# Two early expert tiles in plain float32, and where the split of second weights stands

## The chip, the cores and the metric

The kernel runs on one core of one Trainium2 chip. The metric is the device time of one execution in microseconds (us); lower is better. Of the core's engines the text uses TensorE (PE, with its weight loads PEld), VectorE (DVE), ScalarE (ACT), GpSimd (POOL) and SyncE (SP, which here only issues DMA transfers).

## The reference

Three stages follow each other: a block-causal attention, a dense squared-relu layer, and a mixture of experts that sends each token to one of eight experts. The change lies in the third:

```python
logits = x @ w_gate + modality_bias[modality_id]   # x: 2304 x 512, 8 experts
e_idx = np.argmax(logits, axis=1)
gate_w = probs[np.arange(N), e_idx]                # softmax of logits
for e in range(E):
    mask = e_idx == e
    h = np.maximum(x[mask] @ w1[e], 0.0)           # w1[e]: 512 x 1024, first product
    out[mask] = gate_w[mask, None] * (h @ w2[e])   # w2[e]: 1024 x 512, second product
```

## The kernel before

**Float32 in three products.** Matmuls run on the types `F32` or `F32R`. For most products the kernel splits each float32 operand into a high part (a cast to `F32R`, on ACT) and a low part (the difference, on DVE), and adds up three `F32R` matmuls, high x high, high x low and low x high (`PASSES`, line 498). For a transposed activation `hilo` (924) does this. For weights it is `split` (897), made of `high` (903, ACT, line 904) and `low` (906, DVE, line 910). A whole expert is eight raw weight tiles of 128x1024, `raw[0..3]` for w1 and `raw[4..7]` for w2, each 512 KB. As soon as `low` is through with a raw tile it issues the load of the next token tile's weights into the same place (`load`, 866, on SP's queue). That load has a condition: it moves data only when the next tile has another expert; otherwise it is issued and skipped.

**Token tiles.** The router (`Router`, 501) counts the tokens per expert and packs them into token tiles of 128 rows of one expert. The plan has 17 such tiles (`PLANNED`). The rows that are left over go into six small tiles (32 or 64 rows, `small`, 990), which use plain float32 matmuls and have raw buffers of their own, `raw_s`; their loads are unconditional, and the first tile's eight (`load_small(0, a)`, 887) wait until the gather of the second steady tile has landed (`self.gathered`).

**Two early tiles.** The last block of the dense layer is routed only when its rows are done. Two tiles (`EARLY`, tiles 0 and 1) are chosen before, by `early` (686), from the other tokens of the busiest expert. Their weights are loaded while the dense layer ends: w1 on SP's queue, w2 on POOL's. Then `finish` (747) works out all other tiles on DVE: it ends with `ei` (each tile's expert, 817 and 818), which SP reads before it can issue a conditional load, and `gidx` (the rows to gather, 802), which POOL reads for its gathers (`gather`, 915).

**Order of the work.** `run` (1073) puts the instructions of PE, ACT and DVE in the order in which they are traced (`manual_schedule`); the router's instructions, and those of SP and POOL, are put in between or in order by a scheduler that simulates the kernel. `issue_after(ins)` queues what its block traces on `ins`'s engine behind `ins`; it adds nothing on other engines. The dependency tracker makes a reader of a tile wait for the last instruction before it in traced order that writes the tile, a DMA included.

For the two early tiles `run` splits w1 into high and low, runs tile 0's first product with the matmuls on high weights first (`turns`, 937), lets the parts of the low split wait behind marked points of the router (`acc`, `sel`, `base`, `items`, `index`), runs tile 1's first product, then tile 0's second, then tile 1's second. After them `steady` (1045) works on one tile per turn: first product of tile i, second product of tile i-1, transposes between.

Of the kernel before, what the change touches and what calls it, by code (L numbers as in the profile page):

```python
# [9 lines left out]
F32 = mybir.dt.float32  # L10
# [3 lines left out]
AF = mybir.ActivationFunctionType  # L14
ALU = mybir.AluOpType
AX = mybir.AxisListType
PSUM = bass.MemoryType.PSUM
P = 128
# [260 lines left out]
class SquaredRelu:  # L279
# [54 lines left out]
    def low(self, f, h, l, eng):  # L334
        eng.tensor_sub(l, f, h.bitcast(F32))
# [147 lines left out]
EARLY = 2  # L483
# [14 lines left out]
PASSES = ((0, 0), (0, 1), (1, 0))  # L498


class Router:
# [7 lines left out]
    def __init__(self, nc, persist, ident, modality_id, w_gate, modality_bias, x2_d):  # L509
        self.nc, self.ident, self.x2_d = nc, ident, x2_d  # L510
        NT = x2_d.shape[0]
        D, E = w_gate.shape
        self.NT, self.D, self.E = NT, D, E
        self.NJ = NT // P
        self.NI = NT // P + E - 1
        self.src = (modality_id, w_gate, modality_bias)
        t = lambda n, sh, dt=F32: persist.tile(sh, dt, name=n)
        self.NA = self.NI + TINY + SMALL
        self.gidx = t("gidx", [P, self.NA], I32)
        self.sidx = t("sidx", [P, self.NA], I32)  # L520
        self.ei = t("ei", [1, 2, self.NA], I32)
        self.used = t("used", [1, 1], I32)
        self.gidx_e = t("gidx_e", [P, EARLY], I32)
        self.sidx_e = t("sidx_e", [P, EARLY], I32)
        self.ee = t("ee", [1, 1], I32)
        self.last = {}

    def open(self, ctx, tc, ps, lead):

# [84 lines left out]
    def block(self, blk, rows):  # L614

        nc, E, D, wk = self.nc, self.E, self.D, self.wk
        w = lambda n, sh, dt=F32: wk.tile(sh, dt, name=n, tag=n)
# [33 lines left out]
        oh = self.oh[:, n0:n0 + 2]  # L651
        nc.vector.tensor_tensor(oh, bc(self.down), bc(m2), ALU.is_equal)
        for n in range(2):
            self.last["acc"] = nc.vector.tensor_add(self.acc[:, n0 + n + 1], self.acc[:, n0 + n], self.oh[:, n0 + n])
        yield
        pr = self.ps.tile([P, 2, E], F32, name="pr", tag="g", padded_shape=[P, 64, E])
        nc.tensor.matmul(pr, self.tri, oh, start=True, stop=False)
# [9 lines left out]
        nc.vector.tensor_copy(lo, ri[:, 0])  # L667
        nc.vector.tensor_copy(self.hi[:, n0:n0 + 2], ri[:, 1])
        for e in range(2):
            self.last["sel"] = nc.vector.tensor_scalar(self.A[n0 + e], self.col, lo[:, e:e + 1], None, ALU.is_equal)  # L670
        ex, sm = w("ex", [P, 2, E]), w("sm", [P, 2])
        nc.vector.tensor_sub(ex, lg, bc(m))
        nc.scalar.activation(ex, ex, AF.Exp)
# [73 lines left out]
    def finish(self, ctx, tc):  # L747
# [28 lines left out]
        left = t("left", [P, 1, E])  # L776
        v.tensor_sub(left, tiles, self.less)
        base = self.before("base", left)
        self.last["base"] = v.tensor_scalar_add(base, base, float(EARLY))
        end, zero = t("cend", [P, 1, E]), t("zero", [P, 1, E])  # L780
        v.tensor_add(end, base, left)
        v.tensor_sub(zero, base, self.less)
# [9 lines left out]
        Bm = self.wk.tile([P, NJ, 3, NA], BF16, name="Bm", tag="Bm")  # L792
        v.tensor_tensor(Bm[:, :, 0], self.item.to_broadcast(sh), it.to_broadcast(sh), ALU.is_equal)
        v.tensor_mul(Bm[:, :, 1], Bm[:, :, 0], self.tile_no.to_broadcast(sh))
        self.last["items"] = v.tensor_scalar_mul(Bm[:, :, 2], Bm[:, :, 0], self.part)
        pb = self.ps.tile([P, 3, NA], F32, name="pb", tag="g")
        for j in range(NJ):
            nc.tensor.matmul(pb, self.A[j], Bm[:, j], start=(j == 0), stop=(j == NJ - 1))
        u, w, z = t("tk", [P, NA]), t("tk2", [P, NA]), t("tk3", [P, NA])
        v.tensor_copy(u, pb[:, 2])  # L800
        v.scalar_tensor_tensor(u, pb[:, 1], float(P), u, ALU.mult, ALU.add)
        self.last["index"] = v.tensor_copy(self.gidx, u)
        v.tensor_scalar(w, pb[:, 0], -8192.0, 8192.0, ALU.mult, ALU.add)
        v.tensor_add(z, u, w)
        self.token(self.sidx, z, w)
# [15 lines left out]


class Experts:

# [70 lines left out]
    def split(self, i, a, c, end):  # L897
        if i >= end:
            return
        self.high(a, c)  # L900
        self.low(i, a, c, end)

    def high(self, a, c):
        self.nc.scalar.copy((self.w1s, self.w2s)[a][0][c], self.raw[4 * a + c])  # L904

    def low(self, i, a, c, end, after=None):

        ws, r = (self.w1s, self.w2s)[a], self.raw[4 * a + c]
        with self.tc.issue_after(self.rt.last[after].ins) if after else nullcontext():
            self.nc.vector.tensor_sub(ws[1][c], r, ws[0][c].bitcast(F32))  # L910
        i = max(i + 1, EARLY)
        if i < end:
            self.load(i, a, c)

    def gather(self, i, rows):
        rt, nc = self.rt, self.nc
# [17 lines left out]
            nc.vector.tensor_sub(l[:, s], pt, h[:, s].bitcast(F32))  # L934
        return h, l

    def turns(self, i, n):


        if i == 0:  # L940
            return sorted(((c, a, w) for c in range(n) for a, w in PASSES), key=lambda t: t[2])
        return [(c, a, w) for c in range(n) for a, w in PASSES]

    def hidden(self, i, xT, end):
        nc, KD = self.nc, self.KD
        ph = self.ps_h.tile([P, 2, 512], F32, name="ph", tag="h")
        for t, (c, a, w) in enumerate(self.turns(i, KD)):
            for n in range(2):
                nc.tensor.matmul(ph[:, n], xT[a][:, c], self.w1s[w][c][:, n * 512:(n + 1) * 512],  # L949
                                 start=(t == 0), stop=(t == 3 * KD - 1))  # L950
            if i >= EARLY and t % 3 == 2:
                self.split(i + 1, 0, c, end)
        h = self.hp.tile([P, self.F], F32, name="h", tag="h")
        for n in range(2):
            nc.scalar.activation(h[:, n * 512:(n + 1) * 512], ph[:, n], AF.Relu)
        return h

    def project(self, i, hT, xr, end, between=None):
        nc, D, KF = self.nc, self.D, self.KF
        if i == end - 1:  # L960
            py = self.rt.ps.tile([P, D], F32, name="py", tag="g")
        else:
            py = self.ps_y.tile([P, D], F32, name="py", tag="y")
        for t, (c, a, w) in enumerate(self.turns(i, KF)):
            nc.tensor.matmul(py, hT[a][:, c], self.w2s[w][c // 2][:, c % 2 * D:c % 2 * D + D],  # L965
                             start=(t == 0), stop=(t == 3 * KF - 1))
            if t == 3 * KF // 2 and between:
                between()
            if t % 6 == 5 and i >= EARLY - 1:
                self.split(i + 1, 1, c // 2, end)  # L970
        y = self.sb.tile([P, D], F32, name="y", tag="y")
        nc.scalar.mul(y, py, xr[:, D:D + 1])
        self.scatter(i, y, self.rt.sidx_e if i < EARLY else self.rt.sidx)

    def scatter(self, i, y, idx):
        n = y.shape[0]
# [65 lines left out]
        for j in range(TINY + SMALL):  # L1042
            yield from self.small(j)

    def steady(self, i0, end, xs, xT, before=None, steps=iter(())):

        for i in range(i0, end + 1):
            if i < end:
                h = self.hidden(i, xT.pop(i), end)
            if i == i0 and i + 1 < end and i + 1 not in xT:  # L1050
                xT[i + 1] = self.hilo("x", xs[i + 1], self.KD)
            next(steps, None)
            turn = lambda: self.hilo("h", h, self.KF)
            if before and i == end - 1:
                for _ in steps:
                    pass
                hT = []
                self.project(*before, xs.pop(i - 1), end, lambda: hT.extend(turn()))
                before = i, hT
                continue  # L1060
            if before:
                self.project(*before, xs.pop(i - 1), end)
            for n in range(i + 2, min(i + 4, end)):
                if n not in xs:
                    xs[n] = self.gather(n, self.NT)
            next(steps, None)
            if i < end:
                before = i, turn()
            next(steps, None)
            if i + 2 < end:  # L1070
                xT[i + 2] = self.hilo("x", xs[i + 2], self.KD)

    def run(self):
        nc, tc, KD, KF = self.nc, self.tc, self.KD, self.KF
        i0, end = EARLY, PLANNED
        self.engines = set([mybir.EngineType.PE, mybir.EngineType.Activation, mybir.EngineType.DVE])
        xs, xT = self.xs, {}
        for i in (i0, i0 + 1):
            xs[i] = self.gather(i, self.NT)
        self.gather_small(0)  # L1080
        with tc.manual_schedule(engines=self.engines):
            with tc.high_priority():
                for c in range(4):
                    self.high(0, c)
            xT[0] = self.hilo("x", xs[0], KD)
            for c in range(4):
                self.low(0, 0, c, end, (None, None, "acc", "sel")[c])
            xT[1] = self.hilo("x", xs[1], KD)
            for c in range(4):
                self.high(1, c)  # L1090
            h0 = self.hidden(0, xT.pop(0), end)
            with tc.issue_after(self.rt.last["base"].ins):
                hT0 = self.hilo("h", h0, KF)
            for c in range(4):
                self.low(0, 1, c, end, "index" if c else "items")
            for a in range(2):
                self.load_small(0, a)
            h1 = self.hidden(1, xT.pop(1), end)
            self.project(0, hT0, xs.pop(0), end)
            hT1 = self.hilo("h", h1, KF)  # L1100
            for c in range(4):
                self.split(i0, 0, c, end)
            self.project(1, hT1, xs.pop(1), end, lambda: xT.update({i0: self.hilo("x", xs[i0], KD)}))
            self.steady(i0, end, xs, xT, None, self.smalls())
        self.rest(end, 1)

    def rest(self, i0, n):
# [129 lines left out]
```

## Time and profile before

| | |
|---|---|
| Time, median of 3 runs | 938.98 us (938.69 to 939.5) |
| The profiled execution's own time | 940.87 us |
| Its span in the trace | 939.2 us |
| PE busy | 899.4 us (96%) |
| DVE busy | 600.0 us (64%) |
| ACT busy | 524.1 us (56%) |
| POOL busy | 211.8 us (23%) |

The span runs from the first instruction to the last of one execution; the execution's own time is 1.67 us longer, and 1.89 us above the median of the runs. A busy matmul engine is not one at its peak, since matmuls overlap: a matmul's duration is longer than its distance to the next, and where a rate is wanted, start times are compared.

### The profile page before, as it was taken

Reading aid. Unit: us, or ns where it says so; the run is one execution under the profiler, and the core shown is the slowest. Engines: PE = TensorE matmul, PEld = TensorE weight load, DVE = VectorE, ACT = ScalarE, POOL = GpSimd, SP = SyncE. Lnnn points to the kernel's source line nnn. Section 1 sums busy time; section 2 is a strip of 40 time slices with the busy share of each in tenths; the row PEclk is TensorE's granted clock in tenths of the full one; section 3 lists DMA queues with packets and bytes.
Section 4 is the critical chain, followed back from the end, with each engine's and each line's share of the span. In section 5 each row is a group of like instructions: output and inputs, shape, how many; then the busy total and the mean of one; then the engine's idle time right before and its main releaser. Section 6 shows DMA issues by size and latency. Waiting matters only on the chain. (4 is left out here: it accounts for less than half of the span.)

```text
span 939.2 us, 16334 instructions
## 1 busy us (share of the span) xinstructions
PE 899.4 (96%) x5553; PEld 727.2 (77%) x5553; DVE 600.0 (64%) x1376; ACT 524.1 (56%) x1109; POOL 211.8 (23%) x319
## 2 busy tenths in 40 slices
PE   7989999999999999999999999999889999999995
PEld 5666777787878788999988888887667776766774
DVE  4888876373645445777344444445987887776762
ACT  6878786575756543333222222224377786776763
POOL 4576656133333200000000000002041321222110
PEclk9999999999999999999999999999999999999998
DMA  6465553221321133446012222115173696537400
GB/s 145 133 170 134 161 163 78 76 68 57 73 84 36 50 115 109 135 138 200 23 68 68 69 68 68 46 46 196 52 249 116 231 385 227 210 123 270 159 24 25
DMA packets 109477, 113.79 MB, mean 121 GB/s; under 512 B 62679, under 2 KB 80617, under 8 KB 109387
## 3 DMA queue, kind: packets, MB, share of 16 engines
q1 hardware_dynamic: 105579, 100.74, 34.1%
q0 software_dynamic: 3808, 11.94, 3.6%
q8 instruction: 46, 0.75, 0.3%
q14 instruction: 44, 0.36, 0.1%
HBM read 143.58 MB, written 19.80 MB: 174 GB/s over the span
## 5 line engine op out<-in xcount | busy, mean ns | idle before, releaser
L377 PE MATMUL ph<-xh,wih 128*128 128x256 f32 x576 | 162.9, 283 | 0.0
L377 PE MATMUL ph<-xh,wil 128*128 128x256 f32 x576 | 162.5, 282 | 0.0
L377 PE MATMUL ph<-xl,wih 128*128 128x256 f32 x576 | 162.3, 282 | 0.0
L160 POOL TENSOR_TENSOR p<-p,rc 128x64 f32<-128x64 f32 (+2 forms) x144 | 111.1, 779 | 140.0 <-DVE rc L159 71.2
L381 ACT ACTIVATE r<-ph 128x512 f32<-128x512 f32 x72 | 43.0, 597 | 163.3 <-PE ph L377 138.1
L382 DVE SCALAR_TENSOR_TENSOR r<-r,sc 128x512 f32<-128x512 f32 x72 | 55.8, 775 | 93.6 <-ACT r L381 89.8
L377 PEld LDWEIGHTS ph<-xh,wih 128*128 128x128 f32 x576 | 109.1, 189 | 3.5 <-ACT r L381 0.9
L377 PEld LDWEIGHTS ph<-xl,wih 128*128 128x128 f32 x576 | 109.3, 190 | 2.3
L377 PEld LDWEIGHTS ph<-xh,wil 128*128 128x128 f32 x576 | 109.3, 190 | 0.1
L142 DVE TENSOR_REDUCE nm<-sc 128x1 f32<-128x288 f32 (+8 forms) x160 | 70.7, 450 | 54.8 <-PE sc L140 44.4
L147 ACT ACTIVATE p<-sc,nm 128x288 f32<-128x288 f32 (+8 forms) x160 | 80.4, 505 | 24.2 <-DVE nm L142 10.6
L910 DVE TENSOR_TENSOR w2l<-raw,w2h 128x1024 fp32r<-128x1024 f32 x64 | 77.4, 1223 | 13.9 <-ACT w2h L904 12.8
L910 DVE TENSOR_TENSOR w1l<-raw,w1h 128x1024 fp32r<-128x1024 f32 x64 | 76.8, 1223 | 14.2 <-ACT w1h L904 13.6
L392 PE MATMUL px<-woh,gh 128*128 128x512 f32 x200 | 81.6, 408 | 0.0
L392 PE MATMUL px<-woh,gl 128*128 128x512 f32 x200 | 78.6, 394 | 0.0
L392 PE MATMUL px<-wol,gh 128*128 128x512 f32 x200 | 78.5, 393 | 0.0
L904 ACT CAST w1h<-raw 128x1024 fp32r<-128x1024 f32 x64 | 65.6, 1049 | 16.7 <-PE ph L949 15.3
L919 POOL DMA_INDIRECT xr<-x_d,gidx_e x2 | 2.3, 1129 | 317.0 <-DMA raw<-in_moe_w_dram 316.7
L904 ACT CAST w2h<-raw 128x1024 fp32r<-128x1024 f32 x64 | 66.5, 1049 | 12.4 <-PE py L965 11.3
L385 ACT ACTIVATE gh<-r,sc 128x512 fp32r<-128x512 f32 x72 | 52.2, 725 | 34.1 <-DVE r L382 34.1
L179 PE MATMUL tp<-ident,p 128*128 128x128 f32 x400 | 65.9, 280 | 5.4 <-POOL p L160 3.7
L185 ACT COPY pt<-tp 128x512 f32<-128x512 f32 (+3 forms) x128 | 61.6, 497 | 9.2 <-PE tp L179 8.6
(269 smaller groups left out, 1982.2 us busy)
## 6 DMA issues: line engine op xcount, KB each, us to landing
raw<-in_moe_w_dram SPq DMA_DIRECT2D x172, 512.0 KB
xr<-xT_d SPq DMA_DIRECT2D x19, 512.0 KB
wr<-in_moe_w_in_dram SPq DMA_DIRECT2D x16, 512.0 KB
wr<-in_moe_w_out_dram SPq DMA_DIRECT2D x16, 512.0 KB
row<-part_d SPq DMA_DIRECT2D x20, 256.0 KB
x_d<-row SPq DMA_DIRECT2D x18, 256.5 KB
xT_d<-x SPq DMA_DIRECT2D x16, 288.0 KB
raw_q<-in_q_dram SPq DMA_DIRECT2D x32, 128.0 KB
```

Source lines behind the costliest of these rows:

```text
L142: ps.last["max"] = nc.vector.tensor_reduce(nm[:, e:e + 1], sc[:, 0:w], AX.X, ALU.max, negate=True)
L147: ps.last["exp"] = nc.scalar.activation(pr[:, k0:k0 + w], scs[e][:, 0:w], AF.Exp, bias=nm[:, 0:1], accum_out=sm[:, e:e + 1])
L160: ps.last["scale"] = nc.gpsimd.tensor_mul(pr[:, 0:n], pr[:, 0:n], rc.to_broadcast([P, n]))
L179: nc.tensor.transpose(t[:, e * P:(e + 1) * P], st[u][i][0][:, c * P:(c + 1) * P], ident)
L185: P_COPY(nc, i0)(o, src)
L377: nc.tensor.matmul(ph[:, e], self.wi[p][w][:, c, e * P:(e + 1) * P], x[a][:, c], start=(n == 0), stop=(n == 3 * KC - 1))
L381: nc.scalar.activation(r, ph, AF.Relu)
L382: nc.vector.scalar_tensor_tensor(r, r, self.sc[:, 0:1], r, ALU.mult, ALU.mult)
L385: nc.scalar.activation(gh, r, AF.Identity, bias=self.sc[:, 1:2])
L392: self.nc.tensor.matmul(px, g[a][:, e, t * P:(t + 1) * P], self.wo[p][w][:, e], start=(first and e == 0 and n == 0), stop=(last and e == 1 ...
L904: self.nc.scalar.copy((self.w1s, self.w2s)[a][0][c], self.raw[4 * a + c])
L910: self.nc.vector.tensor_sub(ws[1][c], r, ws[0][c].bitcast(F32))
```

## The change

The classes' parts that mark points in the router (`self.last[...]`) go, except the one behind `gidx`. The core of the rest:

```diff
     def split(self, i, a, c, end):
...
-        self.high(a, c)
-        self.low(i, a, c, end)
...
+        self.nc.scalar.copy(ws[0][c], r)
+        self.nc.vector.tensor_sub(ws[1][c], r, ws[0][c].bitcast(F32))
+        if i + 1 < end:
+            self.load(i + 1, a, c)
...
+    def plain(self, nm, src, n):
+        o = self.sb.tile([P, n, P], F32, name=nm + "f", tag=nm + "h")
+        for g in range(n // 4):
+            pt = (self.ps_t if nm == "h" else self.ps_u).tile([P, 4, P], F32, name="pt" + nm, tag="t")
+            for c in range(4):
+                self.nc.tensor.transpose(pt[:, c], src[:, (4 * g + c) * P:(4 * g + c + 1) * P], self.ident)
+            self.nc.scalar.copy(o[:, 4 * g:4 * g + 4], pt)
+        return o
+
+    def hidden_early(self, xT):
...
+        for c in range(KD):
+            for n in range(2):
+                nc.tensor.matmul(ph[:, n], xT[:, c], self.raw[c][:, n * 512:(n + 1) * 512],
+                                 start=(c == 0), stop=(c == KD - 1))
+        return self.relu(ph)
+
+    def project_early(self, i, hT, xr, between=None):
...
+        for c in range(KF):
+            nc.tensor.matmul(py, hT[:, c], self.raw[4 + c // 2][:, c % 2 * D:c % 2 * D + D],
+                             start=(c == 0), stop=(c == KF - 1))
...
+        self.result(i, py, xr)
...
     def project(self, i, hT, xr, end, between=None):
...
-            if t % 6 == 5 and i >= EARLY - 1:
+            if t % 6 == 5 and i >= EARLY:
                 self.split(i + 1, 1, c // 2, end)
...
     def steady(...):
...
             if i < end:
                 before = i, turn()
+            if i == i0 and w2:
+                for c in range(4):
+                    self.split(i, 1, c, end)
...
     def run(self):
...
-            with tc.high_priority():
-                for c in range(4):
-                    self.high(0, c)
-            xT[0] = self.hilo("x", xs[0], KD)
-            for c in range(4):
-                self.low(0, 0, c, end, (None, None, "acc", "sel")[c])
-            xT[1] = self.hilo("x", xs[1], KD)
-            for c in range(4):
-                self.high(1, c)
-            h0 = self.hidden(0, xT.pop(0), end)
-            with tc.issue_after(self.rt.last["base"].ins):
-                hT0 = self.hilo("h", h0, KF)
-            for c in range(4):
-                self.low(0, 1, c, end, "index" if c else "items")
+            for i in range(2):
+                xT[i] = self.plain("x", xs[i], KD)
+            h0 = self.hidden_early(xT.pop(0))
+            hT0 = self.plain("h", h0, KF)
+            h1 = self.hidden_early(xT.pop(1))
+            for c in range(4):
+                self.load(i0, 0, c)
             for a in range(2):
                 self.load_small(0, a)
-            h1 = self.hidden(1, xT.pop(1), end)
-            self.project(0, hT0, xs.pop(0), end)
+            with tc.issue_after(self.rt.last.ins):
+                for c in range(4):
+                    self.split(1, 1, c, end)
+            self.project_early(0, hT0, xs.pop(0))
             hT1 = self.hilo("h", h1, KF)
             for c in range(4):
                 self.split(i0, 0, c, end)
             self.project(1, hT1, xs.pop(1), end, lambda: xT.update({i0: self.hilo("x", xs[i0], KD)}))
-            self.steady(i0, end, xs, xT, None, self.smalls())
+            self.steady(i0, end, xs, xT, None, self.smalls(), True)
```

Both first products of the early tiles and tile 0's second now take float32 data as it is, from the raw weights and from transposes that ACT alone copies. Tile 1's second product keeps its three matmuls; the split of w2 for it stands ahead of tile 0's second product in the traced order. The split of w2 for tile 2 leaves tile 1's second product and follows the transposes of tile 2's hidden layer.

## Rows read from the trace of the kernel before

**Rows 1.** Busy time in stretches; columns A:B, length, busy (instructions), PEclk, DMA share, GB/s

```profile
664.00:670.00 6.00, 3.81 (x20) 2.60 (x19) 5.69 (x38) 2.48 (x5) 0.00 (x0) 1.00 0.23 88
682.00:688.00 6.00, 5.15 (x18) 3.93 (x19) 3.32 (x7) 3.16 (x5) 3.25 (x4) 0.72 0.43 111
720.00:740.00 20.00, 20.00 (x104) 14.83 (x103) 16.04 (x18) 15.00 (x20) 3.78 (x4) 1.00 0.58 214
```

**Rows 2.** PE in order of time, early tiles; start, duration, line, tiles, count, [idle before]

```profile
656.53 0.66 PE L624 MATMUL gt<-ident,row 128*128 128x128 f32 x4 [0.35 <-DVE row L610]
...
659.55 0.71 PE L949 MATMUL ph<-w1h,xh 128*128 128x512 f32 x2
...
663.74 1.56 PE L949 MATMUL ph<-w1l,xh 128*128 128x512 f32 x6
...
666.80 0.73 PE L949 MATMUL ph<-w1l,xh 128*128 128x512 f32 x2 [1.50 <-DVE w1l L910]
...
669.12 0.71 PE L949 MATMUL ph<-w1h,xh 128*128 128x512 f32 x2
...
674.34 0.63 PE L949 MATMUL ph<-w1h,xl 128*128 128x512 f32 x2
...
678.31 0.96 PE L798 MATMUL pb<-Bm,sel 128*128 128x93 bf16 x18
...
681.12 0.74 PE L965 MATMUL py<-w2l,hh 128*128 128x512 f32 x2 [1.08 <-DVE w2l L910]
...
684.17 1.91 PE L931 MATMUL pth<-ident,h 128*128 128x128 f32 x8
...
685.90 0.80 PE L965 MATMUL py<-w2h,hh 128*128 128x512 f32 x1
...
692.92 0.74 PE L949 MATMUL ph<-w1h,xh 128*128 128x512 f32 x2
...
695.24 0.73 PE L949 MATMUL ph<-w1h,xl 128*128 128x512 f32 x2 [1.11 <-DVE xl L934]
```

**Rows 3.** PE in order of time: plain float32 matmuls of a 64-row small tile

```profile
776.43 3.65 PE L1011 MATMUL phs<-raw,sxT 128*64 128x512 f32 x16
```

**Rows 4.** ACT in order of time, early tiles

```profile
656.22 0.58 ACT L933 CAST xh<-ptx 128x512 fp32r<-128x512 f32 x1 [0.17 <-PE ptx L931]
...
675.06 1.09 ACT L955 ACTIVATE h<-ph 128x512 f32<-128x512 f32 x2 [5.08 <-PE ph L949]
...
686.60 3.89 ACT L904 CAST w1h<-raw 128x1024 fp32r<-128x1024 f32 x4
```

**Rows 5.** DVE in order of time, early tiles

```profile
670.92 0.69 DVE L934 TENSOR_TENSOR hl<-pth,hh 128x512 fp32r<-128x512 f32 x1
...
677.51 1.21 DVE L910 TENSOR_TENSOR w2l<-raw,w2h 128x1024 fp32r<-128x1024 f32 x1
...
679.76 0.18 DVE L802 CAST gidx<-tk 128x31 int32<-128x31 f32 x1
...
687.68 4.63 DVE L910 TENSOR_TENSOR w1l<-raw,w1h 128x1024 fp32r<-128x1024 f32 x4 [0.26 <-ACT w1h L904]
692.23 2.35 DVE L910 TENSOR_TENSOR w2l<-raw,w2h 128x1024 fp32r<-128x1024 f32 x2
```

**Rows 6.** POOL in order of time: the gathers behind gidx

```profile
680.22 1.79 POOL L919 DMA_INDIRECT xr<-x_d,gidx  x1 [26.94 <-DVE gidx L802]
682.32 2.11 POOL L919 DMA_INDIRECT xr<-x_d,gidx  x1 [0.30 <-issue]
```

**Rows 7.** SP's DMA issues in order of time

```profile
677.08 1.87 SPq L861 DMA_DIRECT2D raw<-in_moe_w_dram  x3
...
681.23 1.29 SPq L861 DMA_DIRECT2D raw<-in_moe_w_dram  x2
...
686.71 3.65 SPq L861 DMA_DIRECT2D raw<-in_moe_w_dram  x7
```

**Rows 8.** What SP's queue waited for, 675 to 690 us; us, times, longest

```profile
SPq L861 <- DMA xr<-x_d,gidx: 2.1, 1, 2.1
```

More of the change, by code (lines that the diff above doesn't have):

```diff
@@ L525, in __init__ @@
         self.ee = t("ee", [1, 1], I32)
-        self.last = {}
     def open(self, ctx, tc, ps, lead):
@@ L653, in block @@
         for n in range(2):
-            self.last["acc"] = nc.vector.tensor_add(self.acc[:, n0 + n + 1], self.acc[:, n0 + n], self.oh[:, n0 + n])
+            nc.vector.tensor_add(self.acc[:, n0 + n + 1], self.acc[:, n0 + n], self.oh[:, n0 + n])
         yield
@@ L669, in block @@
         for e in range(2):
-            self.last["sel"] = nc.vector.tensor_scalar(self.A[n0 + e], self.col, lo[:, e:e + 1], None, ALU.is_equal)
+            nc.vector.tensor_scalar(self.A[n0 + e], self.col, lo[:, e:e + 1], None, ALU.is_equal)
         ex, sm = w("ex", [P, 2, E]), w("sm", [P, 2])
@@ L778, in finish @@
         base = self.before("base", left)
-        self.last["base"] = v.tensor_scalar_add(base, base, float(EARLY))
+        v.tensor_scalar_add(base, base, float(EARLY))
         end, zero = t("cend", [P, 1, E]), t("zero", [P, 1, E])
@@ L794, in finish @@
         v.tensor_mul(Bm[:, :, 1], Bm[:, :, 0], self.tile_no.to_broadcast(sh))
-        self.last["items"] = v.tensor_scalar_mul(Bm[:, :, 2], Bm[:, :, 0], self.part)
+        v.tensor_scalar_mul(Bm[:, :, 2], Bm[:, :, 0], self.part)
         pb = self.ps.tile([P, 3, NA], F32, name="pb", tag="g")
@@ L801, in finish @@
         v.scalar_tensor_tensor(u, pb[:, 1], float(P), u, ALU.mult, ALU.add)
-        self.last["index"] = v.tensor_copy(self.gidx, u)
+        self.last = v.tensor_copy(self.gidx, u)
         v.tensor_scalar(w, pb[:, 0], -8192.0, 8192.0, ALU.mult, ALU.add)
@@ L899, in split @@
             return
-        self.high(a, c)
-        self.low(i, a, c, end)
-    def high(self, a, c):
-        self.nc.scalar.copy((self.w1s, self.w2s)[a][0][c], self.raw[4 * a + c])
-    def low(self, i, a, c, end, after=None):
-        ws, r = (self.w1s, self.w2s)[a], self.raw[4 * a + c]
[L909 to L913, printed above, removed]
+        ws, r = (self.w1s, self.w2s)[a], self.raw[4 * a + c]
+        self.nc.scalar.copy(ws[0][c], r)
+        self.nc.vector.tensor_sub(ws[1][c], r, ws[0][c].bitcast(F32))
+        if i + 1 < end:
+            self.load(i + 1, a, c)
     def gather(self, i, rows):
@@ L935, in hilo, with relu, result, turns @@
         return h, l
-    def turns(self, i, n):
-        if i == 0:
-            return sorted(((c, a, w) for c in range(n) for a, w in PASSES), key=lambda t: t[2])
+    def plain(self, nm, src, n):
[7 more added lines that the diff above has]
+    def hidden_early(self, xT):
+        nc, KD = self.nc, self.KD
+        ph = self.ps_h.tile([P, 2, 512], F32, name="ph", tag="h")
+        for c in range(KD):
[4 more added lines that the diff above has]
+    def project_early(self, i, hT, xr, between=None):
+        nc, D, KF = self.nc, self.D, self.KF
+        py = self.ps_y.tile([P, D], F32, name="py", tag="y")
+        for c in range(KF):
+            nc.tensor.matmul(py, hT[:, c], self.raw[4 + c // 2][:, c % 2 * D:c % 2 * D + D],
+                             start=(c == 0), stop=(c == KF - 1))
+            if c == KF // 2 and between:
+                between()
+        self.result(i, py, xr)
+    def relu(self, ph):
+        h = self.hp.tile([P, self.F], F32, name="h", tag="h")
+        for n in range(2):
+            self.nc.scalar.activation(h[:, n * 512:(n + 1) * 512], ph[:, n], AF.Relu)
+        return h
+    def result(self, i, py, xr):
+        y = self.sb.tile([P, self.D], F32, name="y", tag="y")
+        self.nc.scalar.mul(y, py, xr[:, self.D:self.D + 1])
+        self.scatter(i, y, self.rt.sidx_e if i < EARLY else self.rt.sidx)
+    def turns(self, n):
         return [(c, a, w) for c in range(n) for a, w in PASSES]
@@ L946, in hidden @@
         ph = self.ps_h.tile([P, 2, 512], F32, name="ph", tag="h")
-        for t, (c, a, w) in enumerate(self.turns(i, KD)):
+        for t, (c, a, w) in enumerate(self.turns(KD)):
             for n in range(2):
@@ L950, in hidden @@
                                  start=(t == 0), stop=(t == 3 * KD - 1))
-            if i >= EARLY and t % 3 == 2:
+            if t % 3 == 2:
                 self.split(i + 1, 0, c, end)
[L953 to L956, printed above, removed]
+        return self.relu(ph)
     def project(self, i, hT, xr, end, between=None):
@@ L963, in project @@
             py = self.ps_y.tile([P, D], F32, name="py", tag="y")
-        for t, (c, a, w) in enumerate(self.turns(i, KF)):
+        for t, (c, a, w) in enumerate(self.turns(KF)):
             nc.tensor.matmul(py, hT[a][:, c], self.w2s[w][c // 2][:, c % 2 * D:c % 2 * D + D],
@@ L968, in project @@
                 between()
-            if t % 6 == 5 and i >= EARLY - 1:
+            if t % 6 == 5 and i >= EARLY:
                 self.split(i + 1, 1, c // 2, end)
-        y = self.sb.tile([P, D], F32, name="y", tag="y")
-        nc.scalar.mul(y, py, xr[:, D:D + 1])
-        self.scatter(i, y, self.rt.sidx_e if i < EARLY else self.rt.sidx)
+        self.result(i, py, xr)
     def scatter(self, i, y, idx):
@@ L1043, in smalls, with steady @@
             yield from self.small(j)
-    def steady(self, i0, end, xs, xT, before=None, steps=iter(())):
+    def steady(self, i0, end, xs, xT, before=None, steps=iter(()), w2=False):
         for i in range(i0, end + 1):
```

## The prediction

> **What bounds the kernel now.** I read the busy time by stretch first. From 720 us on PE is busy all the time (20.00 of 20 us), at full clock [rows 1]; the query for PE's waits from 705 us to the end names none. So a delay or a gain that still stands when steady work begins, about 700 us, reaches the end whole. The change acts before that, where PE has holes: 3.81 of 6 us from 664, 5.15 of 6 from 682, the last at a mean granted clock of 0.72 [rows 1]. So next I read PE in order of time with what ended each hole [rows 2]: 1.50 us at 666.80 for w1's low split; three holes from 681.12 (1.08 the first) for w2's low split; 1.11 us at 695.24 for tile 2's low half of x, each time behind DVE. Then ACT, DVE, POOL and SP in order of time [rows 4 to 8], to see what the new order would wait for.
>
> **Price of a plain product.** Before, a first or second product is 24 matmuls of 512 columns; tile 1's first goes from 669.12 to 674.97 (last row 674.34 + 0.63) [rows 2], about 0.235 us each, 5.6 us. Plain float32 shows in a small tile: 16 matmul rows in 3.65 us for 8 traced matmuls on two halves of the columns side by side, so each traced matmul is two rows in turn, 3.65/8 = 0.46 with the tail, 0.43 from start to start [rows 3]. No plain product with all 128 columns stands here; I take the same rate, 2 x 0.43 = 0.86 per matmul and 8 x 0.86 = 6.9 us per product. Each product costs PE 1.3 us more than before if nothing waits. Bounds: 3.5 us (one row per matmul) to 7.3 (0.46).
>
> **Tile 0's first product.** It no longer needs the high casts nor the low halves. x of tile 0 is copied by 656.80 [rows 4]; PE then has the router's transposes (656.53 to 657.19 [rows 2]) and tile 1's x, about 0.6: start about 657.8, not 659.55 (bounds 657.2 and 659.5). 6.9 us, plus the router's small matmuls between; the sixteen high matmuls take 4.19 us up to 663.74 [rows 2], 0.46 over 16 x 0.233, and two more groups of the router join them, in all 1.3. End 666.1 with the last one's tail, against 667.53. From there to tile 1's first matmul it is 1.59 us as before (relu, transposes): 667.7. Then 6.9, and perhaps the 18 matmuls of `pb`, which cost 0.8 at 678.31 [rows 2], half of that taken: **end about 675.2**, as good as the 674.97 of before. The gain of the freed DVE is eaten by the dearer products.
>
> **The router's end.** Gone from DVE ahead of `gidx`: four low splits of w1 at 1.21 and four low halves at 0.69 [rows 5], together 7.6 us, of which some lay beside waits for PE or ACT. I take 4.8: `gidx` about 675.1, not 679.94 (bounds 672.3 and 679.9). This moves the gathers too, but PE's next step needs something else.
>
> **The new wait.** Before, tile 0's second product follows at once. After, it reads raw w2, and in the traced order the split of w2 for tile 1, with the conditional load of tile 2's w2 into the same raw tiles, stands ahead of it. So each of its matmuls waits until that load is issued and done, although it moves nothing here: the loads for tile 2 take SP a moment [rows 7], with no traffic behind. Ahead of the load is a chain, all in order on its engines: two relus on ACT (0.1 + 1.09 [rows 4]), the first high cast (about 1.05; four take 3.89 [rows 4]), the low split (0.1 + 1.21 [rows 5]), and SP 0.25 (the split of 677.51 ends at 678.72, the third issue from 677.08 ends at 678.95 [rows 5, 7]). Sum 3.8: the product starts at 679.0, not 675.2. Behind the first the low splits come each 1.2 us, the matmuls on one raw tile take 1.7, so the others don't bind unless SP is late. Were `gidx` at its late bound, the start would be 681.5.
>
> How soon a skipped load signals, no row says. Bounds: nothing, and the 2.3 us from the second gather's end on POOL (684.43) to SP's release at 686.71 [rows 6 to 8]. I take 0.1, since nothing is moved. The Trainium skill, in "DMA: Bandwidth & Descriptors", section "Where the ~2 µs actually goes", puts a transfer's fixed cost at about 2 us, mostly the receipt of the write; no run here shows whether a skipped one pays it. By that page the start would be an estimated 2 us later.
>
> **The clock.** PE now stands still some 4 us. In before, holes of 1.08 us and two shorter ones were followed by a stretch at half clock: 8 transposes spread over 1.91 us at 684.17 and a mean clock of 0.72 in six microseconds [rows 1, 2], that is 0.28 x 6 = 1.7 us lost (half speed is 1.2 GHz of 2.4). I take the same 1.7 here, in the product itself (bounds 0 and 3.4). End: 679.0 + 6.9 + 1.7 = 687.6, where before the transposes of tile 1's hidden layer begin at 684.17: **+3.4**.
>
> **What comes back.** The half clock has moved ahead of those transposes and of tile 1's second product: transposes to first matmul 1.45 instead of 1.73, the product 6.5 instead of 7.02 (685.90 to 692.92 [rows 2]). Tile 2's first product starts at 695.55, +2.6. Its hole of 1.11 us should go: two low splits of tile 2's w2 (2.35 us) stand ahead of the low half of x on DVE [rows 5], and they are moved. DVE then has the four w1 splits from 690.5 to 695.1 and x's low half by 695.8, needed by 696.5. **Net +1.5 us** (own bounds -0.5 and +3).
>
> **The split moved to tile 2** (4 x 1.05 us on ACT, 4 x 1.21 on DVE) costs nothing as long as the first product of tile 3 covers it: from the start of tile 2's first product DVE has 4.9 + 0.7 + 1.3 + 4.9 + 0.7 = 12.5 us of work before w2 is ready, and PE takes some 16 us to come to tile 2's second product. Uncovered it would cost up to 4.9.
>
> **SP's order.** Traced ahead of the four w2 loads are the eight real loads of the first small tile. They wait for the second steady gather, whose landing is 6.8 us after `gidx` (679.94 to 686.71 [rows 5, 7]), so about 682, and take 3.65/7 = 0.52 each [rows 7], 4.2 in all. The w2 loads are ready at 678.7, 679.9, 681.1 and 682.3. SP is not in the hand-ordered set; its order comes from the simulated times, and the last w2 loads are on the edge. With the fourth behind the eight, its matmuls start at 686.9 instead of about 685.9: +1.0. Forecast between the two: **+2.2 us**, in the profiled execution 940.87 + 2.2 = 943.1; against the median of the runs, 938.98 + 2.2 = **941.2**.
>
> **Rivals.**
> *SP's queue holds the product.* Two to four of the w2 loads stand behind the eight real ones. With two behind, the last four matmuls start at 686.5 and end at 689.9: +2.4 over the sum of 1.5, +3.9. With all four behind, the product starts about 686.4, its first matmuls again at half clock, and the third and fourth load share completion signals with real transfers of 512 KB: end about 695, +9. So 943 to 948. For it: traced order and the closeness of 682 to the ready times. Against it: SP's order follows readiness.
> *No wait, hence faster.* If the product doesn't wait for the loads, it runs from 675.2 to 682.1, the splits end beside it (DVE about 682), tile 1's second product ends about 689.5 instead of 692.92, and the 1.11 us hole goes: -4.5, 934.5. It decides at the load's landing: were the raw tiles free before 675. Against it: the traced order puts the load ahead of the reader. With it I count the case that plain products cost 3.5 us (one row per matmul): then `gidx` alone starts the chain and the sum comes to about 935.
> *The moved split is late.* If ACT and DVE pile up in tile 2's turn, PE waits up to 4.9 us there on top of 1.5: 942 to 945.
>
> **How the numbers follow.** A measurement of this kernel can tell about 0.2%, 1.9 us, from no change. Chances: forecast 0.49 (its own range 938.5 to 943: within 0.2% 0.22, slower 0.26, faster 0.01); SP's queue 0.28, slower throughout; no wait or cheap products 0.18, nearly all faster (0.17, and 0.01 within 0.2%); moved split 0.05, slower 0.04, same 0.01. Together faster 0.18, same 0.24, slower 0.58. The range of 8 in 10 is 937 to 948: it takes in SP's queue with all four loads behind, and leaves out most of the fast case.
>
> **What would show it.** The plain products as 16 rows about 0.43 us apart; tile 0's first product starting near 658 and tile 1's ending near 675; `gidx` near 675; tile 0's second product with a hole of about 4 us ahead of it and a DMA or DVE split as its releaser, and a half-clock stretch in it; no hole for x's low half in tile 2's first product. In SP's queue, the place of the conditional w2 loads among the eight real ones. Wrong would be a second product that follows tile 1's first without a hole, holes of over 3 us inside it, or new PE waits after 700 us.

## The result, and the profile after

The changed kernel takes 947.88 us (median of 4 runs, 946.95 to 950.07) against 939.24 for the kernel before, run beside it: a ratio of 1.0093 with a 95% interval of [1.0073, 1.0114], about 8.7 us slower. That lies on the side that was given 0.58, and in the range of 937 to 948, though only by 0.1 us: two of the four runs lie above 948. It is not the forecast of +2.2 but the first rival, SP's queue, at its far end of +9.

PE in order of time after the change, in the columns of [rows 2]:

```profile
657.17 1.02 PE L944 MATMUL ph<-raw,xf 128*128 128x512 f32 x2
...
667.33 7.03 PE L944 MATMUL ph<-raw,xf 128*128 128x512 f32 x16
674.20 0.95 PE L797 MATMUL pb<-Bm,sel 128*128 128x93 bf16 x18
685.67 9.86 PE L952 MATMUL py<-raw,hf 128*128 128x512 f32 x16 [10.52 <-DMA raw<-in_moe_w_dram]
695.37 1.04 PE L922 MATMUL pth<-ident,h 128*128 128x128 f32 x8
696.78 0.50 PE L991 MATMUL py<-w2h,hh 128*128 128x512 f32 x1 [0.38 <-ACT hh L924]
...
703.17 0.63 PE L978 MATMUL ph<-w1h,xh 128*128 128x512 f32 x2
```

The holes behind DVE's splits and behind x's low half [rows 2] are gone; one of 10.52 us stands in their place, ended by a DMA into the raw weights. Behind it the same 16 plain rows that took 7.03 us in tile 1's first product take 9.86. Tile 2's first product starts at 703.17; before it was 692.92, or 694.03 with the 1.11 us hole that now doesn't come: 9.1 us later. The spans of the two traces, 948.4 and 939.2 us, differ by 9.2, so it reaches the end.

The four low splits on DVE, with `gidx` ahead of them, and then SP's issues in three stretches (676 to 680.8: none; then up to 685.3 and up to 690):

```profile
675.64 0.18 DVE L801 CAST gidx<-tk 128x31 int32<-128x31 f32 x1
...
676.51 4.63 DVE L902 TENSOR_TENSOR w2l<-raw,w2h 128x1024 fp32r<-128x1024 f32 x4
```

```profile
680.87 4.23 SPq L861 DMA_DIRECT2D raw<-in_moe_w_dram  x8
685.47 3.11 SPq L861 DMA_DIRECT2D raw<-in_moe_w_dram  x4
```

and what SP's queue waited for from 670 to 692 us:

```profile
SPq L861 <- DMA xr<-x_d,gidx: 4.1, 1, 4.1
SPq L861 <- DMA raw<-in_moe_w_dram: 1.8, 2, 0.9
```

The splits are done at 681.14. SP stands 4.1 us waiting for the second steady gather, issues the eight real loads of the first small tile, and only then the four conditional ones for tile 2, which move nothing; PE's product starts 0.2 us behind the first of these. Twice SP waits 0.9 us more for real loads of 512 KB to complete: in the trace the third and the fourth conditional load wait on semaphores 105 and 106, which are those of the third and the fourth real load. Before [rows 7, 8], the same eight stood behind conditional loads, and no wait of PE from 640 to 705 us is ended by a DMA.

Busy time in three stretches, columns as in [rows 1]:

```profile
674.00:680.00 6.00, 1.16 (x19) 0.80 (x17) 4.56 (x11) 4.85 (x6) 3.29 (x3) 0.80 0.25 74
680.00:686.00 6.00, 0.33 (x1) 0.36 (x2) 1.15 (x2) 0.00 (x0) 1.01 (x2) 0.50 0.77 261
686.00:692.00 6.00, 6.00 (x9) 2.40 (x9) 0.00 (x0) 0.00 (x0) 0.00 (x0) 0.57 1.03 394
```

The clock falls to half in the hole (0.50 from 680 to 686 us), and the product starts at half clock: a mean of 0.57 over six busy microseconds is some 5.2 of them at half (0.43 x 2 x 6).

### The profile page after: what moved, and what is told of

Same layout as the page of the kernel before. It is cut to its first block, busy times and chain, and to the rows that moved or that the text cites. A ratio compares the mean times of both kernels' runs of the same rounds, so it can differ in the third digit from the quotient of the medians.

```text
span 948.4 us, 16273 instructions
## 1 busy us (share of the span) xinstructions
PE 903.2 (95%) x5529; PEld 722.9 (76%) x5529; DVE 593.9 (63%) x1368; ACT 520.2 (55%) x1105; POOL 209.3 (22%) x319
## 5 line engine op out<-in xcount | busy, mean ns | idle before, releaser
L902 DVE TENSOR_TENSOR w1l<-raw,w1h 128x1024 fp32r<-128x1024 f32 x60 | 71.7, 1223 | 15.4 <-ACT w1h L901 14.5
L901 ACT CAST w1h<-raw 128x1024 fp32r<-128x1024 f32 x60 | 61.4, 1053 | 15.4 <-PE ph L978 12.7
```

The lines of the kernel that those rows point to most:

```text
L901: self.nc.scalar.copy(ws[0][c], r)
```

## The experiments

Theory: tile 0's second product waits for SP's queue, where the eight real loads stand ahead. Rivals: the split on ACT and DVE, the plain product itself, the moved split. Each edit is against the changed kernel; ratios are to the kernel before. The stage begins a little earlier or later from run to run, though nothing ahead of it differs: tile 0's first product starts at 657.17 us in the changed kernel and between 655.23 and 657.76 in the eight others. So holes and distances within a trace are compared, not absolute times of two traces.

**The eight loads behind the split.** On SP the four conditional loads then come first.

```diff
-            for a in range(2):
-                self.load_small(0, a)
             with tc.issue_after(self.rt.last.ins):
                 for c in range(4):
                     self.split(1, 1, c, end)
+            for a in range(2):
+                self.load_small(0, a)
```

> The changed kernel with one move: the first small tile's eight loads are traced behind the split of w2 for tile 1, so that on SP the four conditional w2 loads stand ahead of them. Theory (SP's queue holds the product): tile 0's second product starts some 0.3 us behind the first low split's end, about 678 us in place of 685.67, and ends near 686.6; the time falls by 8 to 9 us, to 938.5 to 940.5. Rival (the plain product on raw weights, or the split on ACT and DVE, is the cost): the low splits are where they were, so the time stays at 946 to 949.

Measured: ratio 0.9996 [0.9981, 1.0011], a median of 939.93 us, as the theory had it. The instructions of PE, ACT, DVE and POOL are in the same order; only SP's differ. On SP (two stretches) and PE:

```profile
676.74 3.48 SPq L861 DMA_DIRECT2D raw<-in_moe_w_dram  x4
681.06 4.27 SPq L861 DMA_DIRECT2D raw<-in_moe_w_dram  x8
```

```profile
655.21 0.66 PE L623 MATMUL gt<-ident,row 128*128 128x128 f32 x4 [0.35 <-DVE row L609]
...
656.14 1.02 PE L944 MATMUL ph<-raw,xf 128*128 128x512 f32 x2
...
666.30 7.03 PE L944 MATMUL ph<-raw,xf 128*128 128x512 f32 x16
...
676.93 8.80 PE L952 MATMUL py<-raw,hf 128*128 128x512 f32 x16 [2.80 <-DMA raw<-in_moe_w_dram]
...
685.57 1.04 PE L922 MATMUL pth<-ident,h 128*128 128x128 f32 x8
...
693.39 0.63 PE L978 MATMUL ph<-w1h,xh 128*128 128x512 f32 x2
```

The whole loss of 0.9% goes with the order of SP's queue. What is left is the hole that the forecast was made for, 2.80 us, and a product that takes 1.7 us more than the 7.1 us it takes at full clock (below).

**Half of the eight behind, and the tie to the gather cut.** Two steps between:

```diff
-            for a in range(2):
-                self.load_small(0, a)
+            self.load_small(0, 0)
             with tc.issue_after(self.rt.last.ins):
                 for c in range(4):
                     self.split(1, 1, c, end)
+            self.load_small(0, 1)
```

> The changed kernel with four of the eight real loads (the first small tile's w1) ahead of the split and four (its w2) behind. Theory (each real load ahead costs SP 0.55 us, and the gather's landing near 681 comes first): the product starts near 683.5 in place of 685.7, without waits inside for the loads; with a little less half clock 2 to 3 us less than the change, ratio 1.006 to 1.0075. Rival (any one of them ahead costs as much, since the gather is what counts): ratio 1.008 to 1.0095.

```diff
-            self.fetch(self.raw_s, self.regs["s", j], a, c, nc.sync, self.gathered if j == 0 else None)
+            self.fetch(self.raw_s, self.regs["s", j], a, c, nc.sync)
```

> The changed kernel without the tie that holds the first small tile's loads until the second steady gather has landed; they go out as soon as their expert is known, near 676.6. Theory (of SP's 9 us, 4.3 are that landing, the rest the eight issues): the w2 loads go from about 681, the product starts 4 us earlier; its last parts still wait for completions of real loads; ratio 1.004 to 1.006. Rival (the gather's wait is covered by the split anyway): 1.008 or more.

Measured: 1.0063 [1.0039, 1.0087] and 1.0025 [1.0010, 1.0040]: the first as its theory had it, though its interval reaches into the rival's range; the second better than its theory. PE's row of the product in the one, and with the start of the first product in the other:

```profile
682.45 9.10 PE L952 MATMUL py<-raw,hf 128*128 128x512 f32 x16 [8.77 <-DMA raw<-in_moe_w_dram]
```

```profile
655.23 1.02 PE L944 MATMUL ph<-raw,xf 128*128 128x512 f32 x2
...
678.82 9.31 PE L952 MATMUL py<-raw,hf 128*128 128x512 f32 x16 [5.60 <-DMA raw<-in_moe_w_dram]
```

Time follows the hole: 2.80, 5.60, 8.77 and 10.52 us go with 0.9996, 1.0025, 1.0063 and 1.0093 (the eight loads behind, the tie cut, half behind, the change). In the second kernel the eight loads go out from 673.66, where I took 676.6. Of these 2.9 us 1.9 are the run's own early start (655.23 against 657.17); with the other 1.0 the hole shrinks by 4.9 us where I took 4:

```profile
673.66 4.59 SPq L861 DMA_DIRECT2D raw<-in_moe_w_dram  x8
```

**The hole filled.**

```diff
+            pf = self.ps_h.tile([P, 2, 512], F32, name="pf", tag="h")
+            for n in range(11):
+                nc.tensor.matmul(pf[:, n % 2], hT0[:, 0], hT0[:, 0:4].rearrange("p c t -> p (c t)"), start=True, stop=True)
             self.project_early(0, hT0, xs.pop(0))
```

> The changed kernel with eleven idle plain matmuls of 512 columns ahead of tile 0's second product, into a bank that nobody reads: PE is busy through the hole from about 675.6 to 685, the product still waits for the loads until 685.7. It prices the half clock alone. Theory (the product ran 5.5 us at half clock because of the hole, 2.8 us lost): the product takes 7.0 us in place of 9.86 and the time falls by 2.5 to 3, to 944.5 to 945.5. Rival (the clock follows something else, or plain matmuls don't keep it): 947 to 949.

Measured: 1.0058 [1.0040, 1.0077], 3.3 us under the change by the ratios, where 2.5 to 3 were expected; the two intervals overlap a little, so the size rests on the trace:

```profile
656.13 1.02 PE L944 MATMUL ph<-raw,xf 128*128 128x512 f32 x2
...
674.57 9.71 PE L1124 MATMUL pf<-hf 128*128 128x512 f32 x22 [0.45 <-ACT h L961]
684.63 7.13 PE L952 MATMUL py<-raw,hf 128*128 128x512 f32 x16 [0.36 <-DMA raw<-in_moe_w_dram]
```

```profile
680.00:686.00 6.00, 5.64 (x13) 2.21 (x13) 0.11 (x1) 0.00 (x0) 0.18 (x1) 1.00 0.87 302
686.00:692.00 6.00, 6.00 (x18) 2.81 (x17) 0.00 (x0) 0.19 (x1) 0.00 (x0) 1.00 1.04 395
```

The product waits as long, 28.50 us from the start of the first product in both kernels (684.63 - 656.13, 685.67 - 657.17), but at full clock it takes 7.13 us, not 9.86. Of the change's loss 2.7 us are the clock, the rest is the standstill.

**The split of tile 2's w2 back where it was.**

```diff
-            if t % 6 == 5 and i >= EARLY:
+            if t % 6 == 5 and i >= EARLY - 1:
...
-            self.steady(i0, end, xs, xT, None, self.smalls(), True)
+            self.steady(i0, end, xs, xT, None, self.smalls())
```

> The changed kernel with the split of w2 for tile 2 back in tile 1's second product, as before. Theory (the moved split is covered where it now stands, and was in the way where it stood): two low splits of 1.2 us stand ahead of tile 2's low half of x again, a hole of 1 to 2 us comes back in tile 2's first product: 948.5 to 950. Rival (the moved split costs time in tile 2's turn): 943 to 947. If it is nothing either way: 947 to 948.

Measured: 1.0097 [1.0079, 1.0115], a median of 949.6 us. That is in the theory's range, but the change's interval doesn't tell the two apart. In the trace the hole is back, with the two low splits ahead of x's low half on DVE:

```profile
702.60 2.35 DVE L902 TENSOR_TENSOR w2l<-raw,w2h 128x1024 fp32r<-128x1024 f32 x2
704.87 0.68 DVE L925 TENSOR_TENSOR xl<-ptx,xh 128x512 fp32r<-128x512 f32 x1
```

```profile
705.61 0.73 PE L978 MATMUL ph<-w1h,xl 128*128 128x512 f32 x2 [1.12 <-DVE xl L925]
```

So the move saves PE 1.12 us there, as a row; as a time it is not shown.

**Tile 0's second product in three matmuls.**

```diff
-            hT0 = self.plain("h", h0, KF)
+            hT0 = self.hilo("h", h0, KF)
...
-            self.project_early(0, hT0, xs.pop(0))
+            self.project(0, hT0, xs.pop(0), end)
```

> The changed kernel with tile 0's second product in three matmuls on the split weights as before, so that only the two first products are plain; it reads no raw weights and waits for the split alone. Theory: start near 678, end near 685 with some half clock, ratio 0.997 to 1.0005, though the eight real loads stand ahead in SP's queue as in the change. Rival (the plain first products or the router's order cost time too): 1.003 or more.

Measured: 1.0006 [0.9988, 1.0024]. It waits for no load, though the eight stand ahead in SP's queue as in the change: neither plain first products nor the router's new order cost what the change lost. But it doesn't win either. That a new hole is what keeps it from winning is not shown; at tile 2's hidden layer its trace has one of 2.87 us (next experiment):

```profile
699.57 1.42 PE L922 MATMUL pth<-ident,h 128*128 128x128 f32 x8 [2.87 <-ACT h L961]
```

where the changed kernel has 1.20:

```profile
710.56 1.15 PE L922 MATMUL pth<-ident,h 128*128 128x128 f32 x8 [1.20 <-ACT h L961]
```

**The load behind the product.**

```diff
-    def split(self, i, a, c, end):
+    def split(self, i, a, c, end, load=True):
...
-        if i + 1 < end:
+        if load and i + 1 < end:
             self.load(i + 1, a, c)
...
-                    self.split(1, 1, c, end)
+                    self.split(1, 1, c, end, False)
             self.project_early(0, hT0, xs.pop(0))
+            for c in range(4):
+                self.load(i0, 1, c)
```

> The changed kernel with tile 2's conditional w2 loads traced behind tile 0's second product, which then waits for no load and no split; SP's order is otherwise as it was. Theory: the product follows tile 1's first at about 675.3 us, ends at 682.2 at full clock, and tile 2's first product starts near 690 in place of 703.17: about 13 us less, 934 to 936, below the kernel before. Rival (the product needs the split's time anyway, for the transposes and casts behind it): no better than with the small tile's loads moved, 938 to 941.

Measured: 0.9977 [0.9961, 0.9993], a median of 938.37 us: faster than before, but by 2.2 us, and short of the 934 to 936 that the theory had. The product does start at once. The rest went into another hole. PE, and ACT ahead of it:

```profile
675.58 7.10 PE L952 MATMUL py<-raw,hf 128*128 128x512 f32 x16
...
695.47 0.63 PE L978 MATMUL ph<-w1h,xl 128*128 128x512 f32 x2
...
699.48 1.89 PE L922 MATMUL pth<-ident,h 128*128 128x128 f32 x8 [2.95 <-ACT h L961]
```

```profile
693.54 1.05 ACT L901 CAST w1h<-raw 128x1024 fp32r<-128x1024 f32 x1 [2.32 <-DMA raw<-in_moe_w_dram]
...
698.84 1.08 ACT L961 ACTIVATE h<-ph 128x512 f32<-128x512 f32 x2
```

Tile 3's w1 loads, conditional too, now stand behind the four w2 loads, and those wait for the completions of the eight real ones; SP's waits from 680 to 700 us:

```profile
SPq L861 <- DMA raw<-in_moe_w_dram: 7.5, 5, 2.2
SPq L861 <- DMA xr<-x_d,gidx: 4.3, 1, 4.3
```

On ACT the four late casts stand ahead of tile 2's relu, which starts at 698.84, 2.7 us after PE is through with its input (696.10). PE's hole brings a lower clock: a mean of 0.80 from 696 to 702 us, against 1.00 there in the last kernel below. The three-matmul kernel has the same hole, 2.87 us.

**Both.** The same, and the eight real loads behind the four conditional ones (this edit is against the last kernel):

```diff
-            for a in range(2):
-                self.load_small(0, a)
...
             for c in range(4):
                 self.load(i0, 1, c)
+            for a in range(2):
+                self.load_small(0, a)
```

> The changed kernel with tile 2's conditional w2 loads behind tile 0's second product and the first small tile's eight real loads behind those. Theory (in the run with only the w2 loads moved, they stood behind the eight real loads and tile 3's w1 loads behind them, so the casts of tile 3's w1 held the relu of tile 2: a hole of 2.95 us and a half-clock stretch): that hole shrinks to the 1.2 us of the other kernels, the product still starts at once; tile 2's first product starts near 690; ratio to the kernel before 0.9945 to 0.9965. Rival (the hole is ACT's own pile-up, whatever SP does): it stays, ratio 0.997 to 0.999.

Measured: 935.9 us, ratio 0.9957 [0.9943, 0.9972], which beats both the kernel before and the changed one, as the theory had it. PE:

```profile
674.55 7.10 PE L952 MATMUL py<-raw,hf 128*128 128x512 f32 x16
...
696.68 1.14 PE L922 MATMUL pth<-ident,h 128*128 128x128 f32 x8 [1.20 <-ACT h L961]
```

No hole ahead of the product, and 1.20 us at tile 2's hidden layer, as in the changed kernel. The interval overlaps that of the run with only the w2 loads moved, so what the second move adds rests on this hole (2.95 to 1.20 us) and the clock behind it. With both moves the change is worth 0.4%.

## Why the prediction was right in its range and wrong in its forecast

- **Price of a plain product:** right. 7.03 us with the tail for 16 rows, 6.9 taken.
- **Tile 0's and tile 1's first products:** right. Start 657.17 (657.8), end 674.36 (675.2); `pb` stands behind, not inside. Counted from the router's transposes, whose start moves from run to run, 0.3 us of this is the start and 0.2 the products.
- **The router's end:** right. `gidx` at 675.64 + 0.18 = 675.8 (675.1).
- **The new wait:** the mechanism was right and its last link was not. The chain of relu, cast, split and load shows pure with the eight loads out of the way: hole 2.80, from the first products' end at 673.33 (666.30 + 7.03) to 676.93 it is 3.6 us, 3.8 taken. That a skipped load signals at once was right too: issue 676.74, product 676.93. By the fixed cost of about 2 us in the Trainium skill ("DMA: Bandwidth & Descriptors", section "Where the ~2 µs actually goes", in its part on GpSimd's path; these loads are SP's) the start would be an estimated 678.7. The trace doesn't agree, and for a transfer that moves nothing the measurement decides.
- **SP's order:** the step that failed. The forecast rested on "its order comes from the simulated times, and the last w2 loads are on the edge": at most one of the four behind the eight. All four were behind, in traced order. Moving the eight, or half of them, in the traced order moved them on SP and nothing on the other engines; so the traced order was to be taken as SP's. Why the scheduler keeps it no run shows. The rival's price came out (start 686.4 against 685.67, end 695 against 695.5, +9 against +8.7), in part by errors that offset: the second gather held SP until 5.1 us behind `gidx` (675.82 to 680.87), 6.8 taken, and the half clock cost 1.0 us more than the 1.7 taken. Its chance was too low: 0.28 for all of its cases together, against 0.49 for the forecast. So the range held because the rival's far end was its upper bound, and by 0.1 us that is luck.
- **The clock:** 1.7 us taken for the forecast's hole, 8.80 - 7.1 = 1.7 measured there. With the long hole it is 2.7.
- **What comes back:** right. Transposes to first matmul 1.41 (1.45), tile 1's second product 6.39 (6.5), x's hole gone.
- **The moved split:** covered, as said: behind 712 us PE waits only 0.5 and 0.2 us, for x's low half.
- **Net of the case that was forecast:** +1.5, measured 0.9996, that is -0.4 with an interval of -1.8 to +1.0: about 2 us too dear by the median. The traces have about +0.7, which that interval takes in: from the router's transposes (656.53 before, 655.21 here) to tile 2's first product it is 37.50 us before, with x's hole counted (694.03), and 38.18 here (693.39). So the sum was 0.8 us too dear: 0.3 in the first product's start, 0.2 in the two products, 0.2 in the chain, 0.1 behind. The rest of the 2 us is within what the times can tell.
- **No wait, hence faster:** not what the change does. With both moves it gives 0.9957, 4.0 us less than before, where -4.5 was taken. The first move alone gives 0.9977: the rival left out the loads for tile 3, which stand behind the same queue.

## What to carry to other kernels

When a reader moves from a copy to the buffer that the copy was made from, look at what refills the buffer: if the refill is issued with the copy, the reader waits for the refill, even one that is skipped, and for everything ahead of it in its queue. Where a scheduler orders a queue, as here, count on the order in which it is traced unless a trace shows otherwise, and write down what each item there waits for before an engine on the critical path is tied to it. And when a stall is taken out, look for the next reader behind the same queue: here about half of the gain (2.2 of 4.0 us came first) stayed there until the queue itself was put in order.

## What the runs showed of the hardware that was not expected

- A conditional load that is skipped releases its reader 0.19 us behind the issue's start (676.74 to 676.93), but its turn in the queue can cost microseconds: SP waited 7.5 us in all for completions of real loads ahead of skipped ones (680 to 700 us of the kernel with the load behind the product).
- The half clock outlasts the hole. The product of the changed kernel began at 685.67, and the mean granted clock from 686 to 692 was still 0.57 with PE busy all of it. Matmuls in the hole, whose result nobody reads, kept it at 1.00 and gave the product back 2.7 us.
